# Chunk-selected causal attention and a hard-swish MLP on one core: six head pairs get their scores from two 64-row TensorE tiles and their chunk mask from a VectorE product

## The chip, the cores and the metric

The kernel runs on one core of one Trainium2 chip. The metric is the device time of one execution in microseconds (us), smaller is better. The time before is the median of three runs.

## The reference

For each of 4 batches and 8 heads the reference computes attention of 768 queries with 768 keys, 64 numbers each. The keys lie in 24 chunks of 32. From the minimum and the maximum of each chunk a query gets an upper bound of its scores with that chunk, and only the six causal chunks with the largest bounds, and in them only keys not after the query, take part:

```python
k_min = np.min(k_chunks, axis=3); k_max = np.max(k_chunks, axis=3)
ub = np.sum(np.maximum(q[:, :, :, None, :] * k_min[:, :, None, :, :], q[:, :, :, None, :] * k_max[:, :, None, :, :]), axis=-1)
ub = np.where(causal, ub, -1000000000.0)
top_chunks = np.argsort(ub, axis=-1)[..., -top_k:]          # top_k = 6
sel = (j_chunk == top_chunks[..., None]).any(axis=-2)
mask = sel & (pos[:, None] >= pos[None, :])
attn = softmax(np.where(mask, 0.125 * q @ k.T, -1000000000.0))   # shortened
x = (attn @ v)                                              # as 3072 rows of 512
h = x @ w_in                                                # 512 -> 2048
out = (h * np.clip(h + 3.0, 0.0, 6.0) / 6.0) @ w_out        # 2048 -> 512
```

A query before position 192 has at most six causal chunks, so only the 576 queries from 192 on need a selection.

## The kernel before, in words

**Units of work.** Two heads of a batch make a pair; there are 16 pairs, i = 0 to 15, four per batch. A pair's scores are computed transposed, with keys on the partitions and queries along the row, in six units u = 0 to 5 of one PSUM bank pair each (`UNITS`: a unit lists its pieces as column in the tile, key block j of 128, first query, queries). A unit holds both heads e = 0, 1. In columns for one head the six units have 512, 256, 512, 512, 512 and 384: 2688 in all. The MLP works on groups g = 0 to 7 of 384 rows, half a batch each: eight hidden tokens `H.g.f` (eight matmuls of 384 columns each), then three output tiles `O.g.t`, each in four tokens of four matmuls of 512 columns.

**The order.** The kernel is a list of 1145 tokens, `ORDER`, written out in the source. A loop at the end calls the function of each token. Nothing is scheduled afterwards: every engine, and SyncE's DMA queue, executes its instructions in the order of the list and waits with semaphores where data or a buffer is not ready. The letter at the end of a token (a, b, c, x, y) names the PSUM buffer that it uses; a, b, c are two banks each and are shared by scores and hidden layer.

**Tokens of a pair**, with the lines of the profile:

- loads: `LK LQ LV` (SyncE's queue) and `AK AQ` (ScalarE's queue) load quarters of K, Q, V of a batch 0 pair (L386, 96 KB); `lk lq` load a later pair in four DMAs of 96 KB already laid out for a transpose in 32x32 blocks (L218), and `kd qd` finish that transpose on VectorE (L234, L237). `lv` loads V, `vc VC` cast it to bf16 on GpSimd. `wl wc` load and cast a quarter of a weight (L250) through the two buffers WS.
- `KT QT` (batch 0): TensorE transposes a half of K or Q into PSUM (L397); ScalarE copies it to bf16 (`KB`, L402; `QB`, L405) and makes the positive part of Q in fp32 (`RP`, L419), VectorE the negative part (`RN`, L423; ScalarE for half 1, `RA`, L427), VectorE the chunk maxima and minima (`MX MN`, L409).
- bounds: `UH` or, for two later pairs at once, `ud`, matmuls in 64x32 tiles (L437, L490); `UB us` add the causal bias; then a transpose (`TH`, `tr`), the eight largest of 24 (`T8` L458, `tm` L504), the comparison (`SE` L462, `se` L507) and the transpose back (`LH MT`, `tb` L512). The result is 1 where a chunk is not selected.
- scores `S.i.u`: for pairs 0 to 3 (function `scores`, L537, L542) the two heads are two 64-row tiles, and two small matmuls per piece add -8192 where a chunk is not selected (constant `EM` times the mask). For pairs 4 to 15 (L530) the mask is carried in extra rows of the contraction: head 0 has 96 rows, head 1 has 128, made by `kc`, `qc` (a cast per head: K on GpSimd L306, Q on ScalarE L304), by constant rows written once per buffer (`EK`) and by `mv` (two GpSimd copies per head, L314), which move the mask to where the rows lie.
- `ex`: ScalarE's exp of a unit to bf16 in PT (L548); `af`: GpSimd zeroes the keys after the query in the diagonal blocks, six blocks a pair (L555); `A` and `B.e`: product with V for query blocks 0 to 2 and 3 to 5 (L571; `A` 12 matmuls, each `B` 15); `na nb`: division by the sum of the exps into XB (L588, L591).

**MLP tokens.** The rows of XB are transposed for groups 0 to 2 on TensorE (`X`, L604, six transposes each, copied by VectorE, `xe`, L608) and for groups 3 to 7 by three DMA transposes on SyncE's queue (`xt`, L597). `hu` is ScalarE's relu(h+3) (L623), `gt` VectorE's product with min(.,6) (L626), `ot st` unload (L660) and store (L664) an output tile; the last tile is done in halves (L641, L643).

## Time and profile before

| | |
|---|---|
| median of 3 runs (lowest, highest) | 270.98 us (270.34, 271.39) |
| the profiled execution's own time | 270.87 us |
| its span in the trace | 268.9 us |
| DMA traffic | 35.94 MB, mean 134 GB/s |
| granted TensorE clock | 0.999 of full speed |

All engine shares and durations below come from the one profiled execution; its own time is 1.97 us more than its span. In a row of the trace the count after x is a number of instructions, and the time of a merged row runs from the first start to the last end; matmuls overlap, so what a matmul costs is read from start to start and not from its length. "Idle before, releaser" is what the engine waited for.

### The profile page before, as it was taken

Reading aid. Unit: us, or ns where it says so; the run is one execution under the profiler, and the core shown is the slowest. Engines: PE = TensorE matmul, PEld = TensorE weight load, DVE = VectorE, ACT = ScalarE, POOL = GpSimd, SP = SyncE. Lnnn points to the kernel's source line nnn. Section 1 sums busy time; section 2 is a strip of 40 time slices with the busy share of each in tenths; the row PEclk is TensorE's granted clock in tenths of the full one; section 3 lists DMA queues with packets and bytes.
Section 4 is the critical chain, followed back from the end, with each engine's and each line's share of the span. In section 5 each row is a group of like instructions: output and inputs, shape, how many; then the busy total and the mean of one; then the engine's idle time right before and its main releaser. Section 6 shows DMA issues by size and latency. Waiting matters only on the chain.

```text
span 268.9 us, 6552 instructions
## 1 busy us (share of the span) xinstructions
PE 256.6 (95%) x2492; PEld 156.0 (58%) x2492; DVE 179.4 (67%) x430; ACT 184.1 (68%) x251; POOL 123.3 (46%) x234
## 2 busy tenths in 40 slices
PE   3998989999999999999999999999999999999995
PEld 1665777655455568655555655655555666555544
DVE  2698897889596889988897488746792314632420
ACT  1568899476689898494986588876668796423432
POOL 6901899676857895083392214850325521000000
PEclk9999999999999999999999999999999999999999
DMA  8979895789999928979667437512420021221023
GB/s 167 195 165 169 161 338 111 280 225 324 230 185 194 221 65 143 211 152 204 99 156 160 97 82 174 95 25 58 124 57 2 0 61 41 46 93 39 0 78 117
DMA packets 129102, 35.94 MB, mean 134 GB/s; under 512 B 121776, under 2 KB 122032, under 8 KB 129072
## 3 DMA queue, kind: packets, MB, share of 16 engines
q1 hardware_dynamic: 126672, 34.94, 56.7%
q10 hardware_dynamic: 2400, 0.59, 1.2%
q8 instruction: 19, 0.31, 0.5%
q14 instruction: 11, 0.09, 0.1%
HBM read 27.26 MB, written 6.29 MB: 125 GB/s over the span
## 4 chain that ended last, share of the span: by engine, by line
PE 78%; DVE 6%; ACT 6%; DMA 4%; SPq 2%; issue 2%; POOL 1%; DVEq 0%; ACTq 0%
PE PSx L653 15%; PE PBc L615 11%; PE PBb L615 9%; PE PSy L653 8%; PE PBa L615 8%; PE PBa L530 4%; PE PBb L530 3%; ACT PT L548 3%; PE PBc L530 3%; PE PBa L653 3%; PE PSy L571 2%; PE PSx L571 2%; DMA KSM<-in_k_dram 2%; DMA XT<-XB 2%; ACT U L623 1%
## 5 line engine op out<-in xcount | busy, mean ns | idle before, releaser
L615 PEld LDWEIGHTS <-WIN 128*128 128x128 bf16 x512 | 49.2, 98 | 34.6 <-issue 1.0
L555 POOL TENSOR_SCALAR_AFFINE_SELECT PT<-PT 128x256 bf16<-128x256 bf16 x96 | 37.2, 411 | 52.5 <-ACT PT L548 50.0
L653 PEld LDWEIGHTS <-GT 128*128 128x128 bf16 x368 | 34.7, 97 | 36.2 <-issue 1.5
L653 PE MATMUL PSx<-WOUT,GT 128*128 128x512 bf16 x208 | 51.4, 379 | 0.0
L615 PE MATMUL PBc<-XT,WIN 128*128 128x384 bf16 x200 | 36.6, 326 | 0.3 <-ACT PT L548 0.2
L548 ACT ACTIVATE PT<-PBa 128x1024 bf16<-128x1024 f32 (+2 forms) x35 | 32.2, 919 | 5.9 <-PE PBa L530 5.2
L548 ACT ACTIVATE PT<-PBb 128x1024 bf16<-128x1024 f32 (+2 forms) x32 | 29.3, 916 | 5.3 <-PE PBb L530 4.4
L626 DVE SCALAR_TENSOR_TENSOR GT<-U,PBc 128x768 bf16<-128x768 bf16 x25 | 23.6, 946 | 12.0 <-ACT U L623 11.8
L623 ACT ACTIVATE U<-PBc 128x768 bf16<-128x768 f32 x25 | 20.2, 809 | 16.0 <-PE PBc L615 14.5
L548 ACT ACTIVATE PT<-PBc 128x1024 bf16<-128x1024 f32 (+2 forms) x29 | 27.2, 937 | 5.3 <-PE PBc L530 4.6
L530 PEld LDWEIGHTS <-KB 96*128 96x128 bf16 x240 | 21.4, 98 | 15.5 <-issue 1.6
L615 PE MATMUL PBb<-XT,WIN 128*128 128x384 bf16 x160 | 29.3, 326 | 0.6 <-DMA XT<-XB 0.6
L653 PE MATMUL PSy<-WOUT,GT 128*128 128x512 bf16 x112 | 28.1, 379 | 0.0
L615 PE MATMUL PBa<-XT,WIN 128*128 128x384 bf16 x152 | 27.8, 326 | 0.0
L626 DVE SCALAR_TENSOR_TENSOR GT<-U,PBb 128x768 bf16<-128x768 bf16 x20 | 19.0, 950 | 11.3 <-ACT U L623 11.1
L314 POOL COPY QB<-MTM 32x288 bf16<-32x288 bf16 x48 | 20.2, 421 | 12.9 <-DVE MTM L512 8.3
L571 PEld LDWEIGHTS <-PT 128*128 128x128 bf16 x672 | 23.8, 97 | 3.0 <-issue 0.2
L626 DVE SCALAR_TENSOR_TENSOR GT<-U,PBa 128x768 bf16<-128x768 bf16 x19 | 18.0, 945 | 10.6 <-ACT U L623 10.6
L623 ACT ACTIVATE U<-PBa 128x768 bf16<-128x768 f32 x19 | 15.3, 807 | 13.5 <-PE PBa L615 13.5
L623 ACT ACTIVATE U<-PBb 128x768 bf16<-128x768 f32 x20 | 16.2, 810 | 12.2 <-PE PBb L615 12.0
L362 DVE TENSOR_REDUCE KM<-KSM 128x24 f32<-128x768 f32 x24 | 22.2, 942 | 0.2
L306 POOL CAST KB<-KSM 64x768 bf16<-64x768 f32 x24 | 19.7, 827 | 5.6 <-issue 3.1
(193 smaller groups left out, 385.3 us busy)
## 6 DMA issues: line engine op xcount, KB each, us to landing
out_dram<-OT SPq DMA_DIRECT2D x23, 256.0 KB, 2.4
QS<-in_q_dram SPq DMA_DIRECT2D x61, 96.0 KB, 2.8
KSM<-in_k_dram SPq DMA_DIRECT2D x61, 96.0 KB, 2.8
VS<-in_v_dram SPq DMA_DIRECT2D x12, 384.0 KB, 4.0
WS<-in_moe_w_in_dram SPq DMA_DIRECT2D x4, 1024.0 KB, 7.7
WS<-in_moe_w_out_dram SPq DMA_DIRECT2D x4, 1024.0 KB, 6.2
VS<-in_v_dram SPq DMA_DIRECT2D x16, 96.0 KB, 2.6
KSM<-in_k_dram ACTq DMA_DIRECT2D x3, 96.0 KB, 3.6
```

Source lines behind the costliest of these rows:

```text
L306: engine.tensor_copy(T, src[i % 3][rows])
L314: nc.gpsimd.tensor_copy(aug(QB, i, e)[g:g + CH, Q0 + HQ * h:Q0 + HQ * (h + 1)], MTD[(d // 2) % 2][src:src + CH, e])
L362: nc.vector.tensor_reduce(out=KM[i % 4][:, m, 0:NCH], in_=k_turned(i).rearrange("p (c w) -> p c w", w=CH), axis=AX.X, op=(A.max, A.min)[m] ...
L530: nc.tensor.matmul(PSB[c][:, e, at:at + n], lhsT=K[rows, j * P:(j + 1) * P], rhs=Q[rows, q0:q0 + n], start=True, stop=True)
L548: nc.scalar.activation(PT[i % 3][u][:, :, 0:n], PSB[slot["S", i, u]][:, :, 0:n], ACT.Exp, scale=float(scale))
L555: nc.gpsimd.affine_select(out=T[:, :, lo:lo + P], in_=T[:, :, lo:lo + P], pattern=[[0, 2], [1, P]], compare_op=A.is_ge, fill=0.0, base=0, ...
L571: nc.tensor.matmul(O[:, e, t, :], lhsT=PT[i % 3][u][:, e, lo:lo + P], rhs=VB[i % 4][:, j, e, :], start=(j == 0), stop=(j == qb))
L615: nc.tensor.matmul(PSB[c][:, ff, 0:GRP], lhsT=WIN[:, kt, (2 * f + ff) * P:(2 * f + ff + 1) * P], rhs=XT[g % 3][:, kt, :], start=(kt == 0), ...
L623: nc.scalar.activation(slot["R", g, f][:], PSB[slot["H", g, f]][:, :, 0:GRP], ACT.Relu, bias=3.0)
L626: nc.vector.scalar_tensor_tensor(out=GT[g % 2][:, 2 * f:2 * f + 2, :], in0=slot["R", g, f][:], scalar=6.0, in1=PSB[slot["H", g, f]][:, :, ...
L653: nc.tensor.matmul(PSS[c], lhsT=GT[g % 2][:, f, t * P:(t + 1) * P], rhs=WOUT[:, f, :], start=(f == 0), stop=(f == FT - 1))
```

## The change

1. **Pairs 10 to 15** (the set `PRODUCT`, those that have an `sm` token). `scores` uses the plain K and Q of both heads, one cast of 128 rows each instead of two of 64, and multiplies the two heads as two 64-row tiles at rows 0 and 64, with no mask in the product. `mv` falls away for these pairs. `select_double` now gives 1 where a chunk is selected.
2. **The mask as a product.** `sm.i` stores the small mask of a pair (24 chunks x 2 heads x 576 queries, bf16) to a scratch tensor in DRAM with four DMAs, four copies of each row (0.29 MB). `ml.i.j` loads key block j of it, each row repeated to 32 partitions: 128 partitions of 1152, 1152, 1088, 960, 832, 704 numbers for j = 0 to 5, 1.51 MB a pair; the buffers are two new tiles MX5 (they also hold EM and the identities before) and the two WS, free after the weights. `am.i.j` (j = 2 to 5) zeroes the keys after the query in the diagonal block of the mask on GpSimd, so `af` is left with two blocks for these pairs. `mu.i.u` multiplies PT by the mask on VectorE, piece by piece: per pair four products of 768, four of 256 and two of 384 elements a partition.
3. **Batch 0.** ScalarE copies Q's transposed half to SBUF in fp32 (`QF`) instead of to bf16; GpSimd makes the bf16 Q (`QC`) and the positive part (`PP`) from that copy. `RP` and `QB` fall away.
4. **The order** is another one, of 1210 tokens. What the prediction speaks of: group 2 is turned by `xt.2` and no longer by two `X`; the first score token stands behind all 16 `KT QT` (before: 12), 4 `T8`, 4 `SE`, 6 `UB`, 7 `MX`, 7 `MN`, 2 `MT` (before: 1, 1, 4, 5, 6, 1); ahead of the first hidden token stand eight `B` and three `X` (before four and two); the identity is made ahead of the other constants. After the first hidden token there are 64 `H`, 96 `O`, 72 `S`, 12 `A`, 24 `B`, 6 `ud`, 1 `X` (before 28 `B` and 4 `X`, the others the same). On TensorE the score units of pairs 10 to 15 stand in 15 runs with nothing of another tile shape inside:

```
S.10.0 | S.10.5 | S.10.1 S.11.0 S.11.1 | S.10.2 S.10.4 S.10.3 | S.11.2 S.11.5 | S.11.4 S.11.3 S.12.5 | S.12.1 S.12.0 S.13.4 | S.13.2
S.12.3 S.13.3 | S.12.4 S.13.0 S.12.2 | S.13.1 S.14.0 S.14.1 | S.15.1 S.15.0 S.14.5 | S.14.4 S.15.3 | S.15.2 S.14.3 S.13.5 | S.14.2 S.15.4 S.15.5
```

From `nb.5` to `tb.12` the new list has 16 `H`, 17 `O`, 12 `S` of pairs 4 to 9 and 5 of later ones, 4 `B`, 2 `ud`, 1 `A` for TensorE, and 16 `gt`, 4 `kd`, 4 `qd`, 5 `mn`, 5 `mx`, 4 `kx`, 6 `tm`, 3 `us`, 3 `tr`, 3 `se`, 2 `tb`, 3 `nb`, 1 `na`, 1 `mu` for VectorE. The end of pair 15 reads:

```
ml.15.3 am.15.3 hu.6.4 gt.6.4 gt.6.2 mu.15.2 hu.6.3 gt.6.3 mu.15.5 O.6.2.0.x H.6.6.a O.6.1.1.y O.6.1.2.y B.15.0.c B.15.1.c st.4.2 nb.15 xt.7
H.6.7.b hu.6.7 gt.6.7 O.6.0.0.c O.6.0.1.c O.6.0.2.c O.6.2.1.x O.6.2.2.x hu.6.6 gt.6.6 O.6.1.3.y ot.6.1 O.6.2.3.x ot.6.2 st.6.2 H.7.0.b
```

The core of the diff:

```diff
+    PRODUCT = sorted(named("sm"))
+    MX5 = ring(2, [P, 1856], BF16, "MX5") if PRODUCT else []
+    REP = 4
+    SCR = {i: dram.tile([CH, REP, 2 * NQ], BF16, name=f"SCR{i}") for i in PRODUCT}
...
+    def q_keep(i, h):
+        nc.scalar.copy(QF[i % 3][:, SH * h:SH * (h + 1)], PSS[slot["QT", i, h]][:, 0:SH])
+    def q_half_pool(i, h):
+        nc.gpsimd.tensor_copy(QB[i][:, SH * h:SH * (h + 1)], QF[i % 3][:, SH * h:SH * (h + 1)])
+    def plus_half_pool(i, h):
+        dst, src = part_of(RP, i, h, kept=True)
+        nc.gpsimd.tensor_scalar(out=dst, in0=src, scalar1=1.0, scalar2=0.0, op0=A.mult, op1=A.max)
...
-                                op=A.is_lt)
+                                op=A.is_ge if i in PRODUCT else A.is_lt)
...
+    def mask_store(i):
+        for h in range(2):
+            for e in range(2):
+                g = CH * (2 * (i % 2) + h)
+                nc.sync.dma_start(SCR[i][:, :, NQ * e + HQ * h:NQ * e + HQ * (h + 1)],
+                                  MTD[(i // 2) % 2][g:g + CH, e].unsqueeze(1).to_broadcast([CH, REP, HQ]))
+    def mask_load(i, j):
+        src = SCR[i][4 * j:4 * j + 4].rearrange("c r n -> (c r) n")[:, FIRST[j]:]
+        nc.sync.dma_start(MX[i % 2][j][:, FIRST[j]:], src.unsqueeze(1).to_broadcast([16, 8, 2 * NQ - FIRST[j]]))
+    def mask_apply(i, u):
+        for at, j, q0, n in UNITS[u]:
+            lo = max(q0, Q0)
+            T = PT[i % 3][u][:, :, at + lo - q0:at + n]
+            nc.vector.tensor_tensor(out=T, in0=T, in1=mask_view(i, j, lo, q0 + n), op=A.mult)
...
-                    K, Q = aug(KB, i, e), aug(QB, i, e)
-                    rows = slice(0, P if e else 96)
+                    x = 0 if i in PRODUCT else e
+                    K, Q = aug(KB, i, x), aug(QB, i, x)
+                    rows = slice(e * D, (e + 1) * D) if i in PRODUCT else slice(0, P if e else 96)
+                    at_rows = dict(tile_position=(e * D, 0)) if i in PRODUCT else {}
                     nc.tensor.matmul(PSB[c][:, e, at:at + n], lhsT=K[rows, j * P:(j + 1) * P], rhs=Q[rows, q0:q0 + n],
-                                     start=True, stop=True)
+                                     start=True, stop=True, **at_rows)
...
-            if q0 <= j * P < q0 + n:
+            if q0 <= j * P < q0 + n and not (i in PRODUCT and j * P >= Q0):
```

204 lines of the change are left out of this document (115 added, 89 removed).

## The prediction

> **What bounds the kernel now.** I read the busy shares and the chain of work that ended last, then the busy times by stretch.
>
> ```profile
> PE 256.6 (95%) x2492; PEld 156.0 (58%) x2492; DVE 179.4 (67%) x430; ACT 184.1 (68%) x251; POOL 123.3 (46%) x234
> PE 78%; DVE 6%; ACT 6%; DMA 4%; SPq 2%; issue 2%; POOL 1%; DVEq 0%; ACTq 0%
> ```
>
> ```profile
> 0.00:43.35 43.35, 35.09 (x560) 25.22 (x561) 32.90 (x124) 31.11 (x53) 27.28 (x59) 1.00 0.89 191
> 43.35:265.70 222.35, 221.47 (x1932) 130.74 (x1931) 146.46 (x307) 152.59 (x198) 96.02 (x176) 1.00 0.53 124
> ```
>
> The span is 268.9. The columns are PE, weight loads, DVE, ACT, POOL, clock, DMA share, GB/s. At 43.35 the first hidden token starts, at 265.70 the last matmul has ended, and between them PE is busy for 221.47 of 222.35. A busy PE is not a PE at its peak, so I count its work from start-to-start times in the chain:
>
> ```profile
> 43.35 1.46 PE PBc L615 x8
> 44.81 1.30 PE PBb L615 x8
> 76.29 0.86 PE PSx L653 x4
> 104.32 0.45 PE PBa L530 x4
> 104.77 0.34 PE PSy L604 x6
> 105.11 0.91 PE PSx L571 x30
> 127.70 1.13 PE PBc L490 x32
> ```
>
> A hidden token takes 1.30, an output token 0.864 (0.86 in the row), a score unit of 512 columns 0.45 (two heads, one after the other), an `X` 0.33, a pair of `B` 0.91 (30 ns a matmul), a `ud` 1.13. Behind the first hidden token stand 64 H = 83.2, 96 O = 82.9, 12 pairs of scores at 4 x 0.45 + 0.225 + 0.34 = 2.365, 28.4, 12 A at 0.364 = 4.4, 28 B = 12.7, 6 ud = 6.8 and 4 X = 1.3: 219.7. Of 222.35 that leaves 2.65 without work. **From 43 us on TensorE's work sets the time**, and what is taken off it counts in full while nothing else becomes later. After the last matmul comes a tail of 268.9 - 265.7 = 3.2.
>
> **Scores side by side.** Batch 0 already works in this form, so its price is in the trace:
>
> ```profile
> 98.72 0.61 PE L530 MATMUL PBb<-QB,KB 96*128 96x384 bf16 x4
> 99.17 0.61 PE L530 MATMUL PBa<-QB,KB 96*128 96x384 bf16 x4
> 99.71 0.71 PE L490 MATMUL PBc<-RP,KM 64*32 64x288 f32 x16
> 100.22 0.69 PE L490 MATMUL PBc<-QS,KM 64*32 64x288 f32 x16
> 100.84 0.62 PE L530 MATMUL PBb<-QB,KB 96*128 96x384 bf16 x4
> ```
>
> ```profile
> 30.92 0.25 PE L542 MATMUL PBa<-MTM,EM 64*128 64x96 bf16 x4
> 31.10 0.63 PE L571 MATMUL PSy<-VB,PT 128*128 128x65 bf16 x15
> 31.66 0.34 PE L537 MATMUL PBb<-QB,KB 64*128 64x384 bf16 x2
> 31.83 0.33 PE L542 MATMUL PBb<-MTM,EM 64*128 64x192 bf16 x4
> ```
>
> The two matmuls of 384 columns at 31.66 are done in 0.17, as long as one; four of the old form take 0.45. Six pairs therefore go from 2.365 to 2688 columns at 0.17/384, 1.2 at most, and 1.12 at the rate of the old row's 384+128 columns per 0.225. I take 1.12: -6 x 1.245 = **-7.5**.
>
> The same rows show what a change of tile shape costs. The 15 matmuls at 31.10 need 15 x 0.03 = 0.45, until 31.55, and the next shape starts at 31.66: 0.11. The four of 96 columns at 30.92 need 0.08, until 31.00, and the next shape starts at 31.10: 0.10. Into and out of `ud` it is 0.09 (99.17 + 0.45 to 99.71) and 0.12 (100.22 + 0.50 to 100.84). The new list has 15 runs, so 30 changes at 0.10: **+3.0**; between 1.5, if half of them fall into waits, and 3.6.
>
> The Trainium skill (TensorEngine Tiling (Array Packing), Key Properties) says that a change of tiling mode drains the engine, and its Theoretical Speedup gives up to 2x for a contraction of at most 64 rows; this case's rows show both, the drain as some 0.1. By the 2x alone the scores would give the 7.5; with the drain 4.5 is left.
>
> Group 2's two `X` go: **-0.66**. Two more B pairs (1.82) and one X (0.33) only move ahead of the first hidden token. Work behind it: 219.7 - 7.5 + 3.0 - 0.66 - 2.15 = 212.4.
>
> **The head.** When does the first hidden token start?
>
> ```profile
> 5.72 0.23 DVE L281 CAST IDENTB<-IDENT 128x128 bf16<-128x128 f32 x1 [3.96 <-POOL IDENT masks.py:199]
> 13.66 1.00 DVE L409 TENSOR_REDUCE KM<-PBa 128x12 f32<-128x384 f32 x2
> 16.25 0.87 DVE L458 MAX8 T8D<-PBa 96x8 f32<-96x32 f32 x8
> 19.98 0.27 DVE L462 TENSOR_TENSOR SELD<-PSy,T8D 96x128 bf16<-96x128 f32 x1
> ```
>
> ```profile
> 12.27 0.52 ACT L419 ACTIVATE RP<-PSx 128x384 f32<-128x384 f32 x1
> 12.65 0.51 ACT L405 CAST QB<-PSx 128x384 bf16<-128x384 f32 x1
> 19.48 1.02 ACT L548 ACTIVATE PT<-PBb 128x1024 bf16<-128x1024 f32 x1 [0.93 <-PE PBb L542]
> 44.10 1.01 ACT L548 ACTIVATE PT<-PBa 128x1024 bf16<-128x1024 f32 x1
> ```
>
> The first exp starts at 19.48. In the new list VectorE has more ahead of it: three reductions at 0.5, 16 maxima at 0.11, three comparisons at about 0.3, two bias additions at about 0.45, one copy at 0.2, together 5.3, or about 4.8 as they overlap; the identity comes earlier, which I put at 1.0 of the 3.96 waited for. First exp: about 23.3. From there to the end of the exps ScalarE needed 25.5 (19.48 to 45.0), with eight copies and activations of 0.38 and a cast of 0.8 between. Of these the new list keeps one and an `rp` of about 0.6: 2.8 less, so 46.0. The saved `RP` (eight, about 3.4) lie mostly ahead of the first exp, where ScalarE is not late, and gain little. The last `A` waits for the exp two before the last (-1.6), then come A 0.36, the division 0.75, X 0.33 and its copy 0.5: 46.4, and I take **47.0**, 3.65 later than before, of which 2.15 is the work moved ahead.
>
> GpSimd takes 16 new passes here. Neither is in the trace; one is bounded by nothing (hidden) and twice this cast, since `PP` has two operations:
>
> ```profile
> L391 POOL CAST VB<-VS 128x384 bf16<-128x384 f32 x8 | 4.0, 506 | 7.3 <-DMA VS<-in_v_dram 7.2
> ```
>
> That is at most 16 us on an engine busy for 27.28 of the first 43.35. I take 0, because the list puts `PP` under VectorE's own work; uncovered, one `PP` ahead of each `UH` would add 0.5, 2 over the four pairs. Later GpSimd loses a cast and four moves per pair and ScalarE a cast, off the path both times.
>
> **The mask product.** 60 products on VectorE. The trace has none with two bf16 inputs in SBUF; nearest are a bf16 copy below and products with PSUM or fp32 above:
>
> ```profile
> L608 DVE COPY XT<-PSy 128x768 bf16<-128x768 bf16 x5 | 2.8, 552 | 0.3 <-PE PSy L604 0.3
> L626 DVE SCALAR_TENSOR_TENSOR GT<-U,PBc 128x768 bf16<-128x768 bf16 x25 | 23.6, 946 | 12.0 <-ACT U L623 11.8
> L591 DVE TENSOR_TENSOR XB<-PSy,RINV 128x384 bf16<-128x384 f32 x16 | 8.9, 557 | 0.5
> L462 DVE TENSOR_TENSOR UBT<-PSx,T8D 96x256 bf16<-96x256 f32 x2 | 0.8, 420 | 0.1
> ```
>
> Per pair 4 x 768, 4 x 256, 2 x 384: above 4 x 0.95 + 4 x 0.42 + 2 x 0.56 = 6.6, 39 for six pairs. Below, the copy's rate (0.55 for 768, and 0.29 and 0.35 with the same start cost of 0.15) gives 4.1, 24 for six. I take the copy's, since all operands are 16 bit wide. The Trainium skill (VectorE: DVE Perf Modes, Rules for kernel authors) gives bf16 tensor_tensor 2x; by the cycles of its section Side-by-side 768 elements would take about 0.56, an estimate; no row here shows one.
>
> VectorE's 146.46 of 222 behind the head becomes about 168, on average no bound. One stretch is tight even so, from `nb.5` to `tb.12`:
>
> ```profile
> 100.00:150.00 50.00, 49.98 (x462) 29.82 (x447) 42.28 (x92) 36.18 (x47) 23.18 (x46) 1.00 0.76 151
> L362 DVE TENSOR_REDUCE KM<-KSM 128x24 f32<-128x768 f32 x24 | 22.2, 942 | 0.2
> L234 DVE STREAM_TRANSPOSE KSM<-KSM 128x768 f32<-128x768 f32 x12 | 11.5, 954 | 0.0
> L507 DVE TENSOR_TENSOR SELD<-UBT,T8D 128x576 bf16<-128x576 f32 x6 | 4.6, 764 | 0.1
> ```
>
> Neighbours overlap by about 0.07, so VectorE has there 16 gt and 10 reductions at 0.88, 8 kd and qd at 0.89, six `tm` of nine maxima at 0.9, 11 passes like L507 at 0.7, and 3.6 of divisions and small ones: 46.7. TensorE has 16 x 1.30 + 17 x 0.864 + 12 scores (4.7) + 5 side by side (0.8) + 4 B, 2 ud, 1 A and ten changes (5.5) = 46.5. Before, it lost nothing with VectorE busy for 42.28 of 50; for a VectorE with as much to do as TensorE I add **+1.5** of waits, between 0 and 4.
>
> **The sum.** 47.0 + 212.4 + 2.65 + 1.5 + 3.2 = 266.75 of span; with the 1.97 that the execution has beside it 268.7. Against its own 270.87 that is -2.2; the median is 270.98, so **268.7, 0.8% faster**.
>
> **The rivals.**
>
> *Full relief*: head no later than the moved work (45.5), changes at 1.5, no new waits: 268.7 - 1.5 - 1.5 - 1.5 = 264.2. For: 2.65 of idle behind the head now. Against: the first exp stands behind more VectorE work. 10%.
>
> *The head eats it*: first exp at 25 instead of 23.3, or `PP` uncovered (2): 270.4 to 270.9. For: the DMA share of 0.89 in the head and five more V loads ahead of the first score. 20%.
>
> *VectorE at the upper price*: 15 more. From `nb.4` to `nb.11` its 71 of TensorE's 77.7 become 76, and from `nb.11` to `nb.15` 38 of 54 become 48. Both would stay below, but at 98% and 89%; 3 to 6 of waits: 273. 10%.
>
> *The masks come late* (the slower side). Place: pair 15's last block, `ml.15.3`, on SyncE's queue behind `xt.6`. Its product stands 3.9 of TensorE work ahead of `B.15`, and behind that only 7.3 covers division and transposes of group 7. What that takes now:
>
> ```profile
> 154.23 0.56 DVE L591 TENSOR_TENSOR XB<-PSy,RINV 128x384 bf16<-128x384 f32 x1
> 154.82 3.82 SPq L597 DMA_TRANSPOSE XT<-XB x3
> 161.76 1.46 PE L615 MATMUL PBb<-XT,WIN 128*128 128x384 bf16 x8 [0.56 <-DMA XT<-XB]
> ```
>
> From division to first matmul 7.5, no spare. A block that lands more than 3.9 later than the list has it is paid in full, and the same form stands ahead of groups 4 and 5: three times 2 gives 274.7. For: 10.8 MB of new traffic. Against: a DMA share of 0.53 behind the head. 15%.
>
> *The tiles don't overlap here* (the change doesn't do what it says): -7.5 goes: 276.2. Against: the row at 31.66. 3%.
>
> **Numbers.** Forecast 42% (267.0 to 269.6). Faster by over 0.5%, about what a measurement of this kernel tells from no change (under 269.6): 42 + 10 = 52%. Within: 20%. Slower (over 272.3): 10 + 15 + 3 = 28%. The range reaches from the relief at 264.2 to the late masks at 274.7, and leaves out the last case and the far ends. The forecast's own range is 267.0 to 269.6.
>
> **What would show it.** First hidden token at 46 to 48; first exp near 23; pairs of 64-row matmuls 0.17 apart for 384 columns; 0.1 at a change of shape; mask products of 0.5 to 0.6 for 768; waits of TensorE behind the head of 3 to 5. It is wrong if the first hidden token comes after 49, if a 768 product takes over 0.9, or if TensorE waits for masks or `xt` for more than 3.

## The result, and the profile after

The changed kernel takes 278.24 us (median of 4 runs, 277.57 to 278.98) beside 270.83 for the kernel before (4 runs on the same chip): a ratio of 1.0274, 95% interval 1.0240 to 1.0308, **2.7% slower**. The forecast was 268.7 with a range of 264.2 to 274.7. The profiled execution took 277.57, its span is 275.9. Ratios, here and below, leave out executions that are over 1.5% above the fastest of their kernel, so they are not always the quotient of the two medians.

The busy shares, the granted clock in 40 slices and the chain that ended last, all from the page of the changed kernel:

```profile
PE 254.2 (92%) x2456; PEld 150.8 (55%) x2480; DVE 200.6 (73%) x488; ACT 175.4 (64%) x237; POOL 121.6 (44%) x220
PEclk9968999999999999999999999999999999999999
PE 63%; DVE 9%; DMA 8%; POOL 6%; SPq 6%; issue 3%; ACT 3%; POOLq 0%; DVEq 0%; ACTq 0%
```

TensorE held 78% of the chain before and holds 63% now. What has come in are VectorE, transfers, GpSimd and SyncE's queue. The stretches, with the columns of the prediction's rows, cut just ahead of the first hidden token (53.51) and at the end of the last matmul (272.71):

```profile
0.00:53.40 53.40, 40.60 (x626) 29.16 (x627) 35.42 (x128) 30.32 (x46) 42.91 (x78) 0.94 0.81 179
53.40:272.71 219.31, 213.59 (x1830) 121.60 (x1853) 165.20 (x362) 144.68 (x190) 78.67 (x143) 1.00 0.74 171
```

Most of the miss is in the first row. The head ends at 53.4 where the prediction had 47.0: 6.4 late. Behind it the stretch takes 219.3 where the sum had 216.55 (212.4 of work, 2.65 and 1.5 of waits): 2.75 more. Together 9.15, and with the same tail of 3.2 that is the distance from 266.75 to 275.9. In the head GpSimd is busy for 42.91 (before 27.28) while ScalarE has less to do than before (30.32 after 31.11, in ten more microseconds).

The second row makes TensorE's standing look longer than it was: 219.31 - 213.59 = 5.7, but this trace has recorded only 376 of the 400 matmuls of the output tokens. Below, their group in the changed kernel and, complete, in the kernel "masks first" of the experiments; the last number is the idle time before them:

```profile
L715 PE MATMUL PSx<-WOUT,GT 128*128 128x512 bf16 x194 | 48.7, 379 | 1.1 <-issue 0.5
L713 PE MATMUL PSx<-WOUT,GT 128*128 128x512 bf16 x208 | 50.8, 379 | 0.0
```

Over all buffers these holes make 1.7 (1.1 here, 0.4, 0.1 and 0.1 in the other three), so some 4.0 are real standing.

What TensorE waited for, from the view of waits: target, releaser, then microseconds, times, longest.

```profile
PE PBc L472 <- POOL RP L458: 2.2, 2, 1.3
PE PBa L472 <- POOL RP L458: 2.1, 2, 1.7
PE PBc L677 <- DMA XT<-XB: 1.6, 1, 1.6
PE PBa L633 <- DVE PT L578: 1.6, 2, 1.0
...
PE PBb L472 <- POOL RP L458: 0.6, 1, 0.6
```

L472 are the bounds of batch 0, L458 is `PP`. Five times in the head TensorE stands for GpSimd's positive part, 4.9 us in all. Before, no matmul of the bounds waited for `RP`. Behind the head it stands 1.6 for a mask product (L578, pair 11's first values, L633) and 1.6 for group 4's transposing transfers. Behind the stops in the head the clock is lower; the same columns, by five microseconds:

```profile
10.00:15.00 5.00, 3.23 (x44) 2.22 (x43) 3.41 (x8) 2.19 (x6) 4.79 (x8) 1.00 0.83 187
15.00:20.00 5.00, 4.36 (x44) 2.53 (x44) 2.48 (x9) 2.08 (x5) 2.11 (x3) 0.53 0.71 161
20.00:25.00 5.00, 4.00 (x39) 2.93 (x31) 4.30 (x17) 2.21 (x5) 4.27 (x6) 0.79 0.73 146
```

TensorE is busy for 3.23 of 5 between 10 and 15, and runs at 0.53 and 0.79 of its clock in the next ten (at half from 15.27 to 22.10).

GpSimd's new passes and VectorE's products, groups by shape (busy, mean ns):

```profile
L458 POOL TENSOR_SCALAR RP<-QS 128x384 f32<-128x384 f32 x4 | 6.0, 1492 | 2.5 <-ACT QS L422 2.5
L428 POOL CAST QB<-QS 128x384 bf16<-128x384 f32 x8 | 4.0, 506 | 2.8 <-ACT QS L422 2.8
L458 POOL TENSOR_SCALAR RP<-QS 128x192 f32<-128x192 f32 x4 | 3.4, 851 | 0.5 <-ACT QS L422 0.4
```

```profile
L578 DVE TENSOR_TENSOR PT<-PT,WS 128x768 bf16<-128x768 bf16 x18 | 9.8, 550 | 2.6 <-ACT PT L610 2.6
L578 DVE TENSOR_TENSOR PT<-PT,WS 128x256 bf16<-128x256 bf16 x18 | 5.5, 304 | 0.7 <-POOL WS L571 0.7
L578 DVE TENSOR_TENSOR PT<-PT,MX 128x768 bf16<-128x768 bf16 x6 | 3.6, 608 | 1.9 <-ACT PT L610 1.5 <-DMA WS<-SCR 0.4
```

The cast costs what the old cast of V of the same size did, 506 ns. `PP` from fp32 to fp32 costs 1492 for the same 384 numbers and 851 for half of them. The products come at the copy's price, as forecast. So do the scores side by side, and the late mask stands right behind them (timeline of TensorE: start, length, line, count):

```profile
160.39 0.39 PE L592 MATMUL PBb<-QB,KB 64*128 64x384 bf16 x4
160.62 0.38 PE L592 MATMUL PBa<-QB,KB 64*128 64x384 bf16 x4
160.84 0.38 PE L592 MATMUL PBc<-QB,KB 64*128 64x384 bf16 x4
161.15 0.54 PE L633 MATMUL PSy<-VB,PT 128*128 128x65 bf16 x12
...
164.00 0.20 PE L633 MATMUL PBa<-VB,PT 128*128 128x65 bf16 x1 [0.55 <-DVE PT L578]
165.24 0.48 PE L633 MATMUL PBa<-VB,PT 128*128 128x65 bf16 x10 [1.04 <-DVE PT L578]
```

Four score matmuls (384 and 128 columns, two heads) follow each other at 0.225, where the old form had 0.45, and after the third unit (160.84 + 0.225 = 161.07) the next shape starts 0.08 later. Both are the prediction's prices.

### The profile page after: what moved, and what is told of

Same layout as the page of the kernel before. It is cut to its first block, busy times and chain, and to the rows that moved or that the text cites. A ratio compares the mean times of both kernels' runs of the same rounds, so it can differ in the third digit from the quotient of the medians.

```text
span 275.9 us, 6661 instructions
## 1 busy us (share of the span) xinstructions
PE 254.2 (92%) x2456; PEld 150.8 (55%) x2480; DVE 200.6 (73%) x488; ACT 175.4 (64%) x237; POOL 121.6 (44%) x220
## 4 chain that ended last, share of the span: by engine, by line
PE 63%; DVE 9%; DMA 8%; POOL 6%; SPq 6%; issue 3%; ACT 3%; POOLq 0%; DVEq 0%; ACTq 0%
PE PBa L677 11%; PE PSx L715 10%; PE PBb L677 10%; PE PSy L715 8%; PE PBc L677 8%; SPq L232 3%; DMA VS<-in_v_dram 3%; POOL RP L458 2%; PE PBc L592 2%; DVE PT L578 2%; PE PBb L592 2%; DMA WS<-SCR 2%; PE PSy L633 2%; SPq L400 2%; ACT PT L610 2%
## 5 line engine op out<-in xcount | busy, mean ns | idle before, releaser
L617 POOL TENSOR_SCALAR_AFFINE_SELECT PT<-PT 128x256 bf16<-128x256 bf16 x72 | 28.2, 416 | 22.7 <-ACT PT L610 22.5
L610 ACT ACTIVATE PT<-PBc 128x1024 bf16<-128x1024 f32 (+2 forms) x34 | 31.0, 912 | 5.6 <-PE PBc L592 5.6
L677 PE MATMUL PBa<-XT,WIN 128*128 128x384 bf16 x184 | 33.6, 326 | 0.5 <-DVE XT L670 0.5
L610 ACT ACTIVATE PT<-PBa 128x1024 bf16<-128x1024 f32 (+2 forms) x29 | 27.0, 930 | 7.5 <-PE PBa L592 6.3
L677 PE MATMUL PBc<-XT,WIN 128*128 128x384 bf16 x152 | 27.8, 326 | 1.6 <-DMA XT<-XB 1.6
L633 PEld LDWEIGHTS <-PT 128*128 128x128 bf16 x672 | 23.7, 97 | 7.6 <-DVE PT L578 2.0
L592 PEld LDWEIGHTS <-KB 96*128 96x128 bf16 (+1 forms) x240 | 15.4, 96 | 15.9 <-issue 6.2
L685 ACT ACTIVATE U<-PBc 128x768 bf16<-128x768 f32 x19 | 15.4, 811 | 7.9 <-PE PBc L677 7.8
L688 DVE SCALAR_TENSOR_TENSOR GT<-U,PBc 128x768 bf16<-128x768 bf16 x19 | 17.9, 943 | 3.5 <-ACT U L685 3.4
L336 POOL CAST VB<-VS 128x768 bf16<-128x768 f32 x12 | 10.3, 859 | 21.4 <-DMA VS<-in_v_dram 21.3
L328 POOL COPY QB<-MTM 32x288 bf16<-32x288 bf16 x24 | 10.2, 423 | 20.8 <-DVE MTM L547 19.8
```

The source lines that it names most:

```text
L328: nc.gpsimd.tensor_copy(aug(QB, i, e)[g:g + CH, Q0 + HQ * h:Q0 + HQ * (h + 1)], MTD[(d // 2) % 2][src:src + CH, e])
L336: nc.gpsimd.tensor_copy(VB[i % 4][:, :, :, 0:D], VS[i % 2][:].rearrange("p e j d -> p j e d"))
L592: nc.tensor.matmul(PSB[c][:, e, at:at + n], lhsT=K[rows, j * P:(j + 1) * P], rhs=Q[rows, q0:q0 + n], start=True, stop=True, **at_rows)
L610: nc.scalar.activation(PT[i % 3][u][:, :, 0:n], PSB[slot["S", i, u]][:, :, 0:n], ACT.Exp, scale=float(scale))
L617: nc.gpsimd.affine_select(out=T[:, :, lo:lo + P], in_=T[:, :, lo:lo + P], pattern=[[0, 2], [1, P]], compare_op=A.is_ge, fill=0.0, base=0, ...
L633: nc.tensor.matmul(O[:, e, t, :], lhsT=PT[i % 3][u][:, e, lo:lo + P], rhs=VB[i % 4][:, j, e, :], start=(j == 0), stop=(j == qb))
```

## The experiments

The first table gives what was measured: the median, the ratio to the kernel before on the same chip with its interval, and from the profiled execution the start of the first hidden token, the end of the last matmul, and TensorE's busy time between the two. Before is 43.35, 265.70 and 221.47; after 53.51, 272.71 and 213.59. The last three columns are one execution, which can be 2 us away from the median. A star marks a trace that lacks 22 to 24 matmuls, as that of the changed kernel does; its busy time is some 1.7 low.

| kernel | us | ratio (95%) | first hidden | last matmul | busy between |
|---|---|---|---|---|---|
| batch 0 back | 273.98 | 1.0095 (1.0062 to 1.0128) | 49.16 | 269.65 | 215.36* |
| `PP` with one operation | 277.46 | 1.0237 (1.0195 to 1.0278) | 52.09 | 272.27 | 213.80* |
| GpSimd's part on the old list | 283.82 | 1.0480 (1.0424 to 1.0535) | 58.30 | 281.02 | 220.33* |
| the same, loads moved | 276.01 | 1.0192 (1.0152 to 1.0232) | 48.15 | 270.90 | 221.63 |
| old head | 275.89 | 1.0171 (1.0130 to 1.0213) | 50.50 | 270.99 | 215.43* |
| no product | 272.46 | 1.0027 (1.0000 to 1.0053) | 48.23 | 268.31 | 216.81 |
| full rows | 275.14 | 1.0129 (1.0095 to 1.0163) | 48.10 | 269.31 | 218.66 |
| masks first | 273.37 | 1.0053 (1.0017 to 1.0088) | 48.83 | 267.75 | 215.37 |
| masks and cuts | 274.38 | 1.0114 (1.0076 to 1.0151) | 49.11 | 269.73 | 215.94 |
| cuts behind values | 273.49 | 1.0109 (1.0072 to 1.0145) | 47.85 | 266.45 | 213.42* |
| new list mended | 274.26 | 1.0105 (1.0080 to 1.0130) | 48.80 | 271.59 | 217.49 |
| head of before | 274.22 | 1.0089 (1.0054 to 1.0124) | 43.34 | 269.21 | 219.28 |
| pairs 10 to 15 alone | 278.57 | 1.0267 (1.0236 to 1.0299) | 43.30 | 275.03 | 220.26 |
| the same, full rows | 281.23 | 1.0361 (1.0319 to 1.0404) | 43.22 | 274.77 | 222.87 |
| joint mended | 274.02 | 1.0112 (1.0075 to 1.0150) | 43.53 | 268.73 | 217.85* |
| no masks | 272.37 | 1.0048 (1.0022 to 1.0075) | 43.37 | 267.39 | 217.03* |
| old list, then pairs | 271.45 | 1.0019 (0.9996 to 1.0043) | 43.31 | 268.25 | 219.19 |
| joint and masks again | 273.47 | 1.0094 (1.0057 to 1.0130) | 43.16 | 268.30 | 219.06 |

### GpSimd's part in the head

The theory after the traces: the bounds wait for `PP`, which stands in a ring of TensorE's transpose, ScalarE's copy, GpSimd and TensorE again. The rival: the new order of the head is late by itself.

```diff
-QF.0.0 QC.0.0 PP.0.0
+QB.0.0 RP.0.0            (and so for all eight halves)
```

> The changed kernel with its batch 0 part undone: ScalarE makes the bf16 Q and the positive part from PSUM again (QB and RP in the place of QF; QC and PP gone), everything else and the order as changed. Theory: the head is late because PP takes 0.85 to 1.49 us on GpSimd and every bounds token waits for it, so the first exp moves from 29.6 to 23 to 25 and the time falls to 271.5 to 274. Rival (the new order's loads and VectorE work hold the head): first exp stays after 27.5, time above 276.

Measured 273.98, the first hidden token at 49.2: 4.35 earlier than in the changed kernel, and 1.8% less time (1.0274 to 1.0095). The theory holds for that much. The first exp at 26.1 is later than the 23 to 25 expected, so something else has a share too. In that head the clock still dips, with no GpSimd pass to wait for:

```profile
15.00:20.00 5.00, 3.70 (x47) 2.47 (x38) 4.34 (x21) 3.90 (x12) 0.33 (x1) 1.00 0.65 147
20.00:25.00 5.00, 4.27 (x46) 2.69 (x46) 4.76 (x22) 0.88 (x3) 0.69 (x2) 0.74 0.89 177
```

VectorE has 4.34 and 4.76 of five here. Of TensorE's waits of 0.3 us and more between 10 and 26, 2.0 us are for VectorE's results and 0.4 for ScalarE; then it runs at 0.74.

```diff
-        nc.gpsimd.tensor_scalar(out=dst, in0=src, scalar1=1.0, scalar2=0.0, op0=A.mult, op1=A.max)
+        nc.gpsimd.tensor_scalar(out=dst, in0=src, scalar1=0.0, scalar2=None, op0=A.max)
```

> The changed kernel with PP as one operation (max with 0) on GpSimd instead of two (times 1, max 0). Theory: the second operation is what makes the pass slow; it takes about 0.5 us for 384 elements, like the cast beside it, and the time falls by 2.5 to 4.5, to 274 to 276. Rival: a GpSimd pass from fp32 to fp32 with a scalar costs 1.5 us whatever its operations; time within 1 of 278.2.

Measured 277.46, only 0.8 less (1.0 by the ratios): the rival's bound held. Of that kernel the groups by shape:

```profile
L457 POOL TENSOR_SCALAR RP<-QS 128x384 f32<-128x384 f32 x4 | 4.7, 1163 | 1.1 <-ACT QS L421 1.1
...
L457 POOL TENSOR_SCALAR RP<-QS 128x192 f32<-128x192 f32 x4 | 2.7, 683 | 1.4 <-ACT QS L421 1.3
```

One operation takes 1163 and 683 where two took 1492 and 851: a fifth comes off, and the pass is still over twice the cast of the same size. The second operation was not the price; the pass is. TensorE's waits for `RP` are down from 4.9 to 1.6 us in that trace, and yet the first hidden token comes only 1.4 earlier (52.09): what the view of waits puts down to one releaser is not what its removal brings.

Then this part alone, on the list of before:

```diff
-RP.i.h ... QB.i.h
+QF.i.h ... PP.i.h QC.i.h        (in place of RP and QB of each half)
```

> The kernel before with the batch 0 part alone: QF and QC where QB stood, PP where RP stood (behind its QF), order otherwise as before, no mask product. Theory: GpSimd's positive part delays the head by 3 to 7, time 274 to 278. Rival (the head is late by the new order): within 1.5 of 271.

Measured 283.82, for another computation than the kernel's. In that list pair 3's first Q loads stand ahead of pair 0's copy into the same buffer; the copy waits for them and overwrites them, so pair 3 is computed from pair 0's Q, and TensorE stands 11.3 us for `RP`. The loads were therefore put behind pair 0's passes:

```diff
 QF.0.0 PP.0.0 QC.0.0
+LQ.3.0.1 LQ.3.0.0           (moved from further ahead)
```

> The list of before (all of it, masks on TensorE in pairs 10 to 15 as before) with batch 0's Q kept by ScalarE and its positive part and bf16 form made by GpSimd, each right behind the keeping; pair 3's first Q loads go behind pair 0's, since they share a buffer. The third part of the change alone. Theory: TensorE's bounds wait for GpSimd's two passes (0.85 to 1.5 us for the positive part where ScalarE took about 0.5), each of the first halves later by 1 to 1.5 us in a chain of which two to four steps stand behind each other: the first hidden token goes from 43.4 to 46.5 to 49 and the time up by 1.2 to 2 per cent. Rival, as the prediction had it: ScalarE's lighter load (8 passes of about 0.45 less in the head) pays for it, and the time is within 0.5 per cent of before.

Measured 276.01, +1.9%, the first hidden token at 48.15. Waits of that kernel ahead of it, and its two stretches:

```profile
PE PBb L467 <- POOL RP L453: 2.4, 2, 2.2
PE PBa L467 <- POOL RP L453: 2.3, 2, 1.5
```

```profile
0.00:48.15 48.15, 35.35 (x561) 25.86 (x561) 33.26 (x124) 28.94 (x45) 41.39 (x75) 0.96 0.82 176
48.15:270.90 222.75, 221.63 (x1932) 130.74 (x1931) 146.91 (x307) 152.74 (x198) 95.99 (x176) 1.00 0.53 123
```

The stretch behind the head is that of before (222.75, 222.35). The whole 4.8 us are the head's, and TensorE stands 4.7 for `PP` in it. `PP` takes 1493 and 852 ns there, as in the changed kernel. Put in alone it costs 1.9%, taken out 1.8%: **this part of the change costs 4.8 to 5.2 us**, shown from both sides. ScalarE's relief (28.94 busy after 31.11) pays for nothing.

### The order of the head

```diff
+(the list of before up to its first hidden token, then what is left of the new list)
```

> The mask product with the head of before: the list of before up to its first hidden token, then the rest of the changed list in its own order. It has the old batch 0 part. Theory: the head accounts for about three quarters of the loss; first hidden token at 43 to 44, then 219 to 221.5 as in the changed kernel, time 267.5 to 271. Rival (the mask product itself costs more than it saves): above 273.

Measured 275.89. The first exp was back at 19.2, but the first hidden token came at 50.5: at the joint TensorE stood 3.1 us for a cast of V, which had ended up behind other work on GpSimd. The 267.5 to 271 expected was missed; the time is the rival's, but with that stop in it the run does not show that the mask product is the cause. A later joint, within group 0's hidden tokens:

```diff
+(the list of before up to H.0.5, then what is left of the new list; group 4's masks first, as below)
```

> The kernel's work up to the fourth hidden token in the list of before, word for word (batch 0's Q on ScalarE, the first scores near 19.5 us, the first hidden token near 43.4), then the rest of the new list from there, with group 4's masks ahead as in the run before this one. Theory: the head gives back what the new list lost there, so the first hidden token comes at 43.4 to 44 in place of 49.1. Of B and X the new list had moved 2.15 us ahead of it, that is done behind it again: the stretch behind the first hidden token is 220.5 plus 2 minus 3 of the masks, 219 to 220. Sum 43.5 plus 219.5 plus 3.2 plus 1.2: 266.5 to 268.5, faster than before by 1 to 1.5 per cent. Rival, the two lists do not fit at the joint (loads, casts of weights on GpSimd): TensorE waits there 2 us or more and the time is 269 to 272.

The head came out as expected (43.34), the time did not: 274.22. Behind the head stand 225.9, with 219.28 busy; TensorE lost there 2.4 us for a cut of P on GpSimd, 1.5 for gatings and 1.1 for a normalisation. From the joint on this is the list of "masks first" (below), whose first hidden token comes at 48.83; at group 2's first hidden token the two are level (110.11 and 110.17), and the ratios are 1.0089 and 1.0053. So the lead of 5.5 us is gone by then: 2.15 of it is the moved work, and in this kernel TensorE has five stops up to 69 us, 2.5 in all. This pair does not give a price of the head either.

### The scores of pairs 10 to 15

Their size on TensorE:

```diff
-                    rows = slice(e * D, (e + 1) * D) if i in PRODUCT else slice(0, P if e else 96)
-                    at_rows = dict(tile_position=(e * D, 0)) if i in PRODUCT else {}
+                    rows = slice(0, P) if i in PRODUCT else slice(0, P if e else 96)
+                    at_rows = {}
```

> The order of after with batch 0's Q back on ScalarE; the scores of pairs 10 to 15 multiply all 128 rows for each head instead of its 64, one after the other, so both heads get the sum of the two heads' scores. Theory of the prediction: two 64-row matmuls of 384 columns side by side take 0.17 us where two in a row take 0.33, so 6 pairs lose 6 times 1.25, 7.5 us, and get back 0.1 for each of some 30 changes of shape: the stretch behind the head goes from 220.5 up by 4 to 5, the time to 278 to 279. Rival, a run of 64-row scores pays more than 0.1 at its edges (the weight load ahead of it waits 0.4 us with nothing to wait for, 14 times, 5.8 us): then the side by side form gains next to nothing, and the time stays within 1.5 us of 274.0.

Measured 275.14: by the ratios 0.3% more than with 64 rows (the intervals overlap), where theory wanted 1.5%. But TensorE's busy time is 218.66, and with 64 rows it is 215.37 in "masks first", whose trace is complete too. So the form takes 3.3 off TensorE, and the time shows at most 1 of it. The same edit in another list (below) bears on why, and so does the next run, in which VectorE has nothing to multiply:

```diff
-mu.10.0 ... mu.15.5
```

> The order of after with batch 0's Q back on ScalarE, and the 36 mask products on VectorE left out; the masks are still stored, loaded and cut, so only the selection of chunks in pairs 10 to 15 is missing from the result (and the causal cut of their later blocks, which sits in the mask). Theory: what VectorE pays for the products lies beside TensorE's work and costs nothing by itself; what goes with them is the wait of pair 11's first values for its mask, 2.1 us in two stops, and about 1 us of matmuls at the lowered clock behind it. So the stretch from the first hidden token to the last matmul goes from 220.5 to 217 to 218, and the time from 274.0 to 270.5 to 271.5. Rival, VectorE is the bound of these pairs: 18 products of 0.55 and 18 of 0.3 to 0.4, 16 us, come off the engine that is busy 165 of 220 us, the stretch falls under 216 and the time under 269.5.

VectorE's busy time falls from 164.75 to 143.85, the time by 0.7%, to 1.0027. The expected 270.5 to 271.5 (0.998 to 1.001 of the 271.2 that before took beside the 274.0) was a little low, the rival's under 269.5 is out: VectorE's share is not the bound. That the order in which it gets to its products is, is argued from the waits and not shown by itself. One wait had moved already, 2.3 us for group 4's transfers.

```diff
-ml.11.2 ... ml.10.0 ml.10.2 ... ml.10.5 ... lq.14 ... ml.10.4 ml.10.1 ... ml.11.0 ... ml.11.1
+ml.11.1 ml.10.1 ml.11.0 ml.10.0 ml.11.2 ... ml.10.2 ... ml.10.5 ... lq.14 ... ml.10.4
```

> The order of after with batch 0's Q back on ScalarE, and on SyncE's queue the four mask loads that group 4's first values need (key blocks 0 and 1 of pairs 10 and 11) ahead of the other mask loads, the output store and pair 14's Q loads. Theory: the last of them is then issued near 149 us in place of 156.4, is there near 154, and pair 11's first values (159.7) no longer wait: minus 2.1 of waits and about 1 of lowered clock behind them, plus up to 1 for what the moved loads push back; time 274.0 to 271 to 272. Rival, the masks were late for VectorE too (it is busy 9.1 of 10 us there) or the loads that come later in their place (pair 14's Q, blocks 2) are waited for: the time stays within 1 us of 274.0.

Measured 1.0053, by the ratio 1.1 us less than without the edit: half of what the theory wanted, at the edge of its rival's 1 us, and the intervals overlap. Pair 11's wait for its product fell from 2.1 to 0.2 us, and 1.9 came back elsewhere: GpSimd stood 7.8 us at the cut of block 2, whose load was now a little later, and behind it in its queue stood the casts and cuts that a normalisation hung on. So these were taken out of the way too:

```diff
-am.11.2 ... af.10.0 ... vc.10 ... am.10.2 ... am.10.5 ... af.9.2
+af.10.0 ... vc.10 ... af.9.2 ... am.11.2 am.10.2 am.10.5 mu.10.0     (and ml.11.2 ml.10.2 ahead of the other loads)
```

> The order of after with batch 0's Q back on ScalarE; all six mask loads that group 4's first values need (blocks 2, 1 and 0 of pairs 10 and 11) right behind each other on SyncE's queue, and the three causal cuts of mask blocks on GpSimd put behind the casts and cuts of P of pairs 8 to 10, just ahead of the first product. In the run with the masks first, GpSimd stood 7.8 us at the cut of block 2 with pair 10's V cast and pair 9's cuts behind it, and TensorE then stood 1.9 us for a normalisation of VectorE that hung on them. Theory: with the cuts out of that queue the waits between 150 and 172 us (3.5 to 4 us of idle, and the lowered clock) fall under 1.5: the ratio to before goes from 1.0053 (masks first) and 1.0095 (batch 0 back alone) to 0.995 to 1.001. Rival: VectorE's own queue is late there, the products come at their old time, and the ratio stays at 1.003 or over.

1.0114; the rival held, though not for the cause that it named. GpSimd and TensorE of that kernel:

```profile
162.05 0.41 POOL L569 TENSOR_SCALAR_AFFINE_SELECT WS<-WS 128x256 bf16<-128x256 bf16 x1 [2.34 <-DMA WS<-SCR]
162.41 1.25 POOL L615 TENSOR_SCALAR_AFFINE_SELECT PT<-PT 128x256 bf16<-128x256 bf16 x3
```

```profile
163.72 0.54 PE L631 MATMUL PBa<-VB,PT 128*128 128x65 bf16 x12 [2.99 <-POOL PT L615]
```

GpSimd waits 2.34 for a mask block (10.4) that nobody needs yet, and pair 11's own cut of P stands behind it in the queue.

```diff
-am.10.5 ... af.10.1 am.10.4 ... af.11.0
+af.10.1 ... af.11.0 am.10.5 am.10.4
```

> As the run with masks and cuts moved, with two more cuts of mask blocks (10.5 and 10.4) put on GpSimd behind pair 11's last cut of P, so that no cut of P that group 4's first values wait for stands behind a mask that has not landed. Theory: the 3.0 us for which TensorE stood there for a cut of P behind block 10.4's cut, and about 1 us of lowered clock behind it, go: ratio to before from 1.0114 to 0.998 to 1.003. Rival: the next late one is VectorE (its queue holds the products in order) and the ratio stays at 1.006 or over.

1.0109; expected was 0.998 to 1.003. The 3.0 us at GpSimd were gone in the trace, whose run was the fastest of six (271.36, the others 272.6 to 275.7) and the only one at the full clock, so it does not show what the others lost. In their place stood 1.9 for group 4's transfers, behind pair 15's Q loads on SyncE's queue, and 1.2 for a gating behind a product.

### Pairs 10 to 15 without the rest

```diff
+(the list of before up to group 2's first hidden token, then what is left of the new list, masks and cuts as above)
```

> The list of before, word for word, up to group 2's first hidden token (near 124 us; batch 0 as in before, first hidden token near 43.4), and from there the rest of the new list with the masks and cuts placed as in the run beside this one: what is left of the change is pairs 10 to 15. Theory: those pairs give TensorE 6 x 1.25 = 7.5 us less and 3 us of changes of shape more; against the full-row run busy time differed by 3.3, so 3.3 to 4.5 come off before's 222.35 behind the head, less 1 to 2 for what is left of waits for masks: ratio to before 0.985 to 0.995. Rival: the freed time is eaten by VectorE's products and the masks' loads wherever the head stands: ratio 0.997 or over.

> The same kernel as the one before it, with all 128 rows for each head in the scores of pairs 10 to 15, so both heads get the sum of the two heads' scores: the gain of the side by side form alone, in a list where little waits for masks. Theory: TensorE busy 3.3 to 4.5 us longer behind the head, and the time too, by 1.2 to 1.7 per cent. Rival: waits take what the smaller work leaves, and the two kernels are within 0.5 per cent.

1.0267 and 1.0361. The first is no verdict on the pairs: the joint left pair 10's K load late, VectorE stood 8.1 us for it, and TensorE behind it:

```profile
118.49 2.72 PE L675 MATMUL PBc<-XT,WIN 128*128 128x384 bf16 x8 [8.02 <-DVE XB L651]
121.01 2.61 PE L675 MATMUL PBa<-XT,WIN 128*128 128x384 bf16 x8
123.45 1.46 PE L675 MATMUL PBb<-XT,WIN 128*128 128x384 bf16 x8
```

The stall is paid twice: 8.0 us of standing, and two hidden tokens at 2.5 in place of 1.3, counted from start to start. The two kernels have it alike, so their difference still says what the form is worth: 0.9%, and 2.6 us of busy time.

> As the run of pairs 10 to 15 alone, with pair 10's K loads put ahead at the joint and its turn and reduces on VectorE behind pair 6's normalisation (there VectorE stood 8.1 us for that load, TensorE 8.0 behind it, with the clock at half for the next 10 us), and the mask cuts as in the run beside this one. Theory: some 10 us of that run's 278.0 span were the joint's, 1 to 2 the cuts': span 265.5 to 267.5, ratio to before 0.988 to 0.996. Rival: what pairs 10 to 15 gain on TensorE is taken by their masks in this list too: ratio 0.999 or over.

> The kernel with the joint mended, with the whole mask path of pairs 10 to 15 left out: no stores and loads of masks, no cuts of them, no products, so these pairs select no chunks and their later blocks are not cut causally. Theory: where the masks' path is hidden in the list of the run beside it, this one gains under 1 us on it; what is left of waits goes: ratio 0.984 to 0.990. Rival, the mask path is the price of the form: 3 us or more under the run beside it.

```diff
-st.1.1 lk.10 st.1.2 kd.10 mn.10 ... mx.10 kc.10 B.7.0.c B.7.1.c kx.10 nb.7
+lk.11 lk.10 ... B.7.0.c B.7.1.c nb.7 ... nb.6 kd.10 mn.10 mx.10 kx.10 ... kc.10
```

The second leaves out the whole mask path besides (`sm`, `ml`, `am` and `mu` of these pairs). 1.0112 and 1.0048, both above what was expected. In both, pair 13's K went into the buffer ahead of pair 10's turn, so pair 10 is computed with pair 13's K and its turn waits for that load: TensorE stood 4.4 and 4.9 us at the joint. The second is 0.6% under the first, 1.7 us for the whole mask path, stores, loads, cuts and products (the intervals just touch); neither "under 1" nor "3 or more".

```diff
+lk.13 behind xt.3 ... xt.4 lq.15
```

> The list of before up to group 2's first hidden token, the rest of the new list behind it (masks and cuts as in the last runs), with the joint in the right order: pair 10's K is loaded, turned and reduced before pair 13's K goes into the same buffer (the run with the mended joint, and the one without masks, had pair 13's K in pair 10's place there, and its turn stood for that load), and pair 15's Q loads behind group 4's transposing transfers on SyncE's queue (they held them up by about 3 us, and TensorE then stood 1.9 us for them). Theory: the joint's 4.4 us and about 1.5 of lowered clock behind it go from a span of 271.7, and 1 to 2 at group 4: 264.5 to 266.5, ratio to before 0.983 to 0.993, so that pairs 10 to 15 by themselves do gain. Rival: what they free on TensorE goes into waits wherever the list is joined; ratio 0.999 or over.

> The new list with batch 0's Q back on ScalarE, masks and cuts as in the last runs, and pair 15's Q loads behind group 4's transposing transfers. Theory: it only takes the 1.9 us wait off, so ratio 1.000 to 1.006, and it stays behind the run beside it by the 4 to 5 us by which its head is later (first hidden token near 48.5 against 43.4) less the 2 us of B and X that it has done by then. Rival: the ratio is that of the run beside it within 0.4 per cent, and the head costs nothing.

**1.0019 (0.9996 to 1.0043)** and 1.0105 (1.0080 to 1.0130). The first has the list of before up to group 2 and pairs 10 to 15 in the new form behind it, and it takes as long as the kernel before: the rival held. The second missed its 1.000 to 1.006, and its 0.86% (2.3 us) over the first is not shown to be the price of the new head. From group 3's first hidden token on the two lists are the same, token for token, and there the new list is ahead (the first kernel's row, then the second's):

```profile
130.58 1.46 PE L675 MATMUL PBc<-XT,WIN 128*128 128x384 bf16 x8
129.13 1.46 PE L675 MATMUL PBc<-XT,WIN 128*128 128x384 bf16 x8
```

What the new list loses on the first in these traces (last matmul at 271.59 and 268.25) it loses behind that point. The first one's stretches and its stop at the joint:

```profile
0.00:43.31 43.31, 35.07 (x560) 24.84 (x561) 32.82 (x124) 31.02 (x53) 26.34 (x58) 1.00 0.86 189
43.31:268.25 224.94, 219.19 (x1932) 125.02 (x1931) 170.27 (x367) 147.00 (x192) 84.09 (x147) 0.99 0.72 171
```

```profile
119.51 2.30 PE L675 MATMUL PBa<-XT,WIN 128*128 128x384 bf16 x8 [2.50 <-DVE GT L686]
121.60 1.91 PE L713 MATMUL PSx<-WOUT,GT 128*128 128x512 bf16 x4
```

TensorE has 2.3 us less to do than before (221.47) and stands 5.75 us (224.94 - 219.19) where it stood 0.88. At group 4 it stood 1.8. In the second, TensorE stood 3.8 us at group 4: with pair 15's Q loads now ahead of an output store, ScalarE waited 4.5 us for that store's buffer, and the relus behind it in its queue, and with them VectorE's gatings, were late. Both traces are of long executions for their kernels (272.94 is the second longest of 12, 276.46 the longest of 6).

> As the run of the old list and then the pairs, with what its two stops showed put right: at the joint pair 10's K is loaded some 15 us earlier and turned in a gap of VectorE before group 2, its reduces stand behind the gatings that group 2's next hidden token waits for (TensorE stood 2.5 us there and had the clock at 0.83 for 10 us), pair 10's bounds stand one half score later; and block 3 of pair 11's mask is loaded ahead of group 4's transposing transfers, its product behind group 4's second gating (TensorE stood 1.8 us there). Theory: about 4 us of the 271.45 come off, 266.5 to 268.5, ratio to before 0.984 to 0.992: pairs 10 to 15 gain 1 to 1.5 per cent where nothing else of the change is there. Rival: VectorE has no room for pair 10's work at the joint and for the products behind it, the stops only move, and the ratio stays within 0.4 per cent of 1.

```diff
-lk.10 ... kd.10 mn.10 mx.10 kx.10 ... gt.2.4
+lk.10 (15 us earlier) ... kd.10 nb.7 ... gt.2.4 ... gt.2.5 mn.10 mx.10 kx.10 ... ml.11.3 xt.4 ... mu.11.3 mu.11.5
```

1.0094: not the theory's gain, and further from 1 than the 0.4% of the rival. What the rival said of the stops is in the trace: the stop of 2.5 at the joint was gone and one of 2.6 stood 6 us later, for pair 10's bf16 Q on ScalarE, behind VectorE's turns:

```profile
125.35 0.61 PE L591 MATMUL PBb<-QB,KB 64*128 64x384 bf16 x4 [2.63 <-ACT QB L317]
130.73 1.46 PE L676 MATMUL PBc<-XT,WIN 128*128 128x384 bf16 x8 [1.00 <-DVE UBM L529]
```

No list was found here in which the pairs gain. Whether one exists is left open.

## Why the prediction was wrong, step by step

- **What bounds the kernel** and the tail of 3.2: right.
- **"I take 0, because the list puts `PP` under VectorE's own work"**: this step failed, and it is half of the miss: 4.8 to 5.2 us (out: 1.8%; alone: 1.9%) of the 9.5 between 268.7 and 278.24. By itself it would have turned the sign. Without it the change is still 0.95% slower where 0.8% faster was forecast, so the steps below failed too, by some 4.7 together. The bound beside it failed as well. "Twice this cast" is 1.01 for 384 numbers; `PP` takes 1.49, and 0.85 for half of that. And "uncovered, one `PP` ahead of each `UH` would add 0.5, 2 over the four pairs" priced the difference of two operations and left out that `QF` stands ahead of `PP`: where ScalarE's `RP` (0.33 for 192 numbers, 0.50 for 384) was read straight from PSUM, there are now a copy (0.48) and then 0.85 or 1.49, 1.0 to 1.5 more in each turn of the ring. Five waits of 4.9 us in all, and a clock of 0.53 and 0.79 behind them, are what the trace shows of it. The copy's row and its consumer were both in the prediction; the chain from one to the other was not followed.
- **First exp 23.3, first hidden token 47.0**: late without GpSimd too, 24.3 to 26.1 and 47.9 to 49.2 in the seven kernels with the new head and the old batch 0. The stretch from one to the other was right (23.7 forecast, 22.4 to 24.6 measured). In four of the seven the clock was at half for 3.41 us ahead of it, and the first exp came at 25.7 to 26.1; in the three where it stayed full, at 24.3 to 25.1. So 1.0 to 1.8 is the estimate's own, and for the rest it had no term. The first hidden token is 4.5 to 5.8 later than before, less the 2.15 of moved work 2.4 to 3.7, where 1.5 was forecast. What of this reaches the end of the kernel no pair of runs here isolates.
- **Scores side by side, -7.5, changes of shape +3.0**: right in both prices (0.225 for 0.45; 0.08 to 0.1 a change), and the net of 4.5 was 3.3 by the busy time (218.66 less 215.37) and 2.6 in the other list. With -0.66 and -2.15 the work behind the head fell by 6.1 (221.47 to 215.37), forecast 7.3.
- **The mask product at the copy's price**: right, 550 to 608 for 768. By the Trainium skill (VectorE: DVE Perf Modes, Rules for kernel authors) bf16 `tensor_tensor` runs at 2x; the trace agrees, 550 ns beside 946 for the gating of as many numbers, which reads PSUM.
- **+1.5 of waits**: too little. Behind the head TensorE stood some 4.0, and 0.88 before by the same two columns (222.35 - 221.47): 3.1 more, where 1.5 was added. The place was not the tight stretch of VectorE but group 4's masks, one of the three places of the rival "the masks come late", which had it at 274.7 and 15%; its first place, pair 15's last block, did not show up. In the changed kernel it was 1.6 us of standing, not three times 2; with the 1.6 for `xt.4` it is just over the 3 that the prediction named as a sign of being wrong.
- **Pairs 10 to 15 as a whole**: forecast at -4.5 + 1.5, measured at +0.2% (interval 0.0 to +0.4) behind the old list, in a kernel that has a stop of 2.5 us of its own at the joint. That what comes off TensorE "counts in full while nothing else becomes later" was the condition, and it did not hold: in each list tried, TensorE stood for another engine or queue instead.

By the ratios, 1.8% of the 2.7% is GpSimd's part. The other 0.95% lies in the new order and the pairs together; how it splits between them is not shown.

## What to carry to other kernels

When work moves from one engine to another inside a chain (transpose, copy, positive part, bounds), price the whole way round for the consumer, with the new pass taken from a row of the same operation and types and never from a cast; how busy the two engines are did not tell it here. In a list written out by hand each engine and each queue is a line of its own: a wait put into one of them (a mask cut, a load, a store) holds up everything behind it, so list what stands behind before moving a token. Where TensorE was busy 221 of 222 us, taking 3 us of work off it bought nothing in any list tried here, since its suppliers had not been made earlier. And the price of a late start is read at a point from which two lists are the same, not at the start: the new list is behind by 5.5 us at the first hidden token and ahead by 1.5 at group 3.
